# Making P and Q of chunk 5 behind the last stage of chunk 0 instead of behind its first

## The chip, the cores and the metric

The kernel runs on one core of a Trainium2 chip. The metric is device time in microseconds of one launch, the median of the runs shown. In the text PE is TensorE, DVE is VectorE, ACT is ScalarE, POOL is GpSimd, and SP is SyncE, which here does nothing but issue DMAs.

## The reference

Three parts follow one another. The first is a recurrence over 768 time steps with a 40x40 state for each of 32 heads (4 batches of 8), the second and the third are two feed-forward blocks over the 3072 tokens.

```python
for t in range(S):
    y[:, :, t] = np.einsum('bhd,bhde->bhe', rt, state)
    Sa = np.einsum('bhde,bhe->bhd', state, at)
    state_decay = state * wt[:, :, None, :] - np.einsum('bhd,bhe->bhde', Sa, bt)
    state = state_decay + np.einsum('bhd,bhe->bhde', vt, kt)
...
h = (x @ w1) * (x @ w2) @ w3      # moe:  3072x320, 320x1024, 1024x1024
x = h @ w_out                     #       1024x320
out = np.maximum(x @ w_in, 0) ** 2 @ w_out2   # moe2: 320x2048, 2048x320
```

## The kernel before

**The recurrence in chunks.** The 768 steps are cut into 24 chunks of 32 (C = 32). What a chunk needs that does not depend on the state is prepared ahead, mostly six chunks ahead, and what depends on the state is a chain of stages, one chunk after the other.

The preparation of chunk p has three steps. `prep` (L819) loads a tile `im` with k, b and a of the chunk and a tile `iw` with its decays, runs two scans on DVE (`suf`, L556, and `wi`, L566) and multiplies their results into `im` (L578 and L584, on POOL from chunk 4 on). `prep_pq` (L588), called "pq" in the tables, makes P and Q: 32 matmuls over `im` into a PSUM tile `pat` (L597), a copy of P by ACT into `Pn` (L601), a transpose of Q by DVE into `qt` (L602), a mask by POOL (L604) and a store to `Q_d` in DRAM (L605). `prep_kb` (L607), "kb", transposes k and b on PE (L614), copies them on ACT to `kn` (L618) and stores them in `KB_d` (L619). The tiles `im` (except chunks 1, 2, 3 and 5), `iw`, `suf`, `wi`, `qt` and `kn` exist once, so the next chunk waits until the last reader of the one before is done. Four chunks together then go through a triangular solve on DVE (L656, L659).

The chain of chunk c is `do_x0` (PE L742, copy to X0 by ACT L744), `do_sa` (PE L752, ACT L754), `do_sat` (PE L759, ACT L764 and L761, which write `YI` and `vs`), `do_l` (PE L772, DVE L777 writes `YI`), for c > 0 `do_z` (PE L785, ACT L788 writes `YR`), and `do_ys` (PE L800 in two halves). `do_ys` ends on DVE: L808 writes the new state into `RX`, on which the next chunk's `do_x0` waits, and L812 writes the output. For the first four chunks the solve works on halves of 16 steps, and `corner` (PE L690 and L693, ACT L697 and L701) completes the inverse. All PSUM tiles of the chain and of the preparation rotate over two buffers of the name `pat`.

**Filling.** Between the stages PE gets independent work from a queue: the product of w3 and w_out ("fold", L462, into `pw`), then the first feed-forward block (L370, L428), and at the end the weights of the second block. The weights come as 64-bit words and are decoded: a DMA to a tile `raw` or `early` (L319, 512 KB each), two passes on ACT (L325 and L326), two on DVE (L328 and L330), and for w1 and w2 also a cast on ACT (L340) and a difference on POOL (L341). Of `raw` there are three buffers, of the decoded w1 and w2 tiles (`wst`, tag "split") two, and the `early` tiles are two pairs that are used twice.

**What sets the order.** On PE the order is that in which the code is written (manual_schedule). On ACT, DVE, POOL and SP a scheduler decides, from the priorities that the code gives and from a timeline of its own in which it plays the kernel; each engine then takes its instructions strictly in that order. So the place of a PE instruction can move instructions on the other four engines. Which preparation stands between which stages of the first four chunks is in the table BETWEEN (L32): a key is a chunk and the stage behind which the listed steps are called (by `more`, L881, through `run`, L846).

Of the kernel before, what the change touches and what calls it, by code (L numbers as in the profile page):

```python
# [30 lines left out]
)  # L31
BETWEEN = {  # L32
    (0, "start"): (("prep", 5), ("prep", 6)),
    (0, "x0"): (("corner", 0), ("pq", 5)),
    (0, "sat"): (("corner", 1, 0),),
    (0, "l"): (("corner", 1, 1),),
    (0, "ys"): (("kb", 5), ("pq", 6), ("kb", 6)),
    (1, "start"): (("prep", 7),),
    (1, "sat"): (("corner", 2, 0),),
    (1, "l"): (("corner", 2, 1),),  # L40
# [1096 lines left out]
```

## Time and profile before

| | us |
|---|---|
| median of 3 runs | 1073.65 (1069.87 to 1074.45) |
| profiled execution, its own time | 1071.28 |
| its span, first to last instruction | 1069.5 |
| PE busy in the span | 918.1 (86%) |
| DVE busy | 712.5 (67%) |
| ACT busy | 443.8 (41%) |
| POOL busy | 233.2 (22%) |

The mean clock granted to PE is 0.961 of full speed. The chain that ended last goes for 48% of the span over PE, for 26% over DVE and for 12% over DMAs. The kernel has three parts in time: to about 59 us only preparation, to about 690 us the 24 chunks with the filling between them, and from about 740 us the second feed-forward block, in which PE is busy almost all the time. The change lies at the start of the second part.

How to read it: an engine's row gives the start, the duration, the line, and out<-in by the names in the code; in brackets stands how long the engine was idle before it and what ended that. An idle engine costs time only where the chain waits for it.

### The profile page before, as it was taken

The page shows a single profiled execution, that of the slowest core. Times are in us where ns is not written, and L with a number is a line of the kernel's source. Part 1 is how long each engine was busy: PE and PEld are TensorE (multiplying, and loading weights), DVE is VectorE, ACT ScalarE, POOL GpSimd, SP SyncE. Part 2 cuts the span into 40 slices and gives each one's busy share as a digit, 9 for nine tenths or more (in the row PEclk, how much of TensorE's full clock was granted, in tenths as well). Part 3 has the DMA queues.
Part 4 walks back from the last instruction along what each step waited for, and adds up shares of the span by engine and source line. Part 5 has one row for each costly group of instructions (what it writes and reads, how often), then busy time and mean ns, then how long its engine had stood idle before and what let it go on. Part 6 is the DMA issues. An engine that isn't in the chain of part 4 may idle for free.

```text
span 1069.5 us, 29225 instructions
## 1 busy us (share of the span) xinstructions
PE 918.1 (86%) x12240; PEld 822.5 (77%) x12240; DVE 712.5 (67%) x1399; ACT 443.8 (41%) x942; POOL 233.2 (22%) x304
## 2 busy tenths in 40 slices
PE   1327777688989889979899999889999999999997
PEld 1315545588888878979798889868989898898896
DVE  6864879957975997798489444887456554444432
ACT  2424556343434423424343434775334333333332
POOL 0271224433343343533200000652000000000000
PEclk9999888899999999989899999989999999999999
DMA  8976785666666567766644542665122121000001
GB/s 212 307 235 177 209 247 158 171 168 170 163 154 173 148 151 182 170 170 149 164 118 110 136 96 60 171 188 111 30 62 53 59 48 25 2 25 1 18 8 28
DMA packets 208922, 134.45 MB, mean 126 GB/s; under 512 B 143741, under 2 KB 184062, under 8 KB 208368
## 3 DMA queue, kind: packets, MB, share of 16 engines
q1 hardware_dynamic: 201424, 110.61, 40.6%
q0 software_dynamic: 7072, 21.57, 7.1%
q8 instruction: 99, 1.62, 0.7%
q10 hardware_dynamic: 288, 0.33, 0.2%
q14 instruction: 39, 0.32, 0.1%
HBM read 99.27 MB, written 33.19 MB: 124 GB/s over the span
## 4 chain that ended last, share of the span: by engine, by line
PE 48%; DVE 26%; DMA 12%; issue 5%; ACT 4%; POOL 3%; SPq 2%; ACTq 0%; DVEq 0%; POOLq 0%
PE ph L370 16%; PE po L997 15%; PE ab L370 6%; DMA im<-img 5%; DVE tmp L656 4%; PE px L428 4%; DVE T L659 4%; PE pat L800 2%; DVE RX L808 2%; DVE yst L812 2%; DVE gl L408 2%; DVE g L402 1%; DVE wst L328 1%; DVE YI L777 1%; POOL im L584 1%
## 5 line engine op out<-in xcount | busy, mean ns | idle before, releaser
L997 PE MATMUL po<-wul,rh 128*128 128x320 f32 x384 | 118.3, 308 | 0.0
L997 PE MATMUL po<-wuh,rh 128*128 128x320 f32 x384 | 118.0, 308 | 0.0
L997 PE MATMUL po<-wuh,rl 128*128 128x320 f32 x384 | 116.9, 308 | 0.0
L407 ACT CAST gh<-g 128x256 fp32r<-128x256 f32 x96 | 39.0, 406 | 99.8 <-DVE g L402 86.5
L370 PE MATMUL ph<-xh,wih 128*128 128x512 f32 x192 | 76.0, 396 | 0.7 <-issue 0.7
L428 PE MATMUL px<-wph,gh 128*128 128x320 f32 x192 | 68.1, 355 | 9.3 <-DVE x L433 4.8
L370 PE MATMUL ph<-xh,wil 128*128 128x512 f32 x192 | 75.7, 394 | 0.0
L370 PE MATMUL ph<-xl,wih 128*128 128x512 f32 x192 | 75.6, 394 | 0.0
L997 PEld LDWEIGHTS po<-wul,rh 128*128 128x128 f32 x384 | 72.0, 188 | 4.2
L997 PEld LDWEIGHTS po<-wuh,rh 128*128 128x128 f32 x384 | 72.0, 188 | 3.8
L997 PEld LDWEIGHTS po<-wuh,rl 128*128 128x128 f32 x384 | 71.6, 188 | 0.6 <-DVE rl L984 0.6
L800 PE MATMUL pat<-YI,YR 128*40 128x72 f32 (+1 forms) x1536 | 58.8, 240 | 13.7 <-DVE qt L602 8.1
L800 PEld LDWEIGHTS pat<-YI,YR 128*40 128x40 f32 x1536 | 54.5, 127 | 19.2 <-DVE qt L602 9.7
L408 DVE TENSOR_TENSOR gl<-g,gh 128x256 fp32r<-128x256 f32 x96 | 48.2, 503 | 30.0 <-ACT gh L407 29.6
L401 ACT COPY a_sb<-ab 128x256 f32<-128x256 f32 x96 | 35.6, 371 | 76.4 <-PE ab L370 75.9
L656 DVE TENSOR_TENSOR tmp<-PT,T 128x31 f32<-128x31 f32 (+20 forms) x170 | 64.9, 382 | 3.4
L659 DVE TENSOR_TENSOR T<-T,tmp 128x31 f32<-128x31 f32 (+20 forms) x170 | 64.5, 380 | 3.0
L428 PE MATMUL px<-wph,gl 128*128 128x320 f32 x192 | 63.2, 329 | 3.4 <-DVE gl L408 3.4
L584 POOL TENSOR_TENSOR im<-im,suf 104x256 f32<-104x256 f32 x80 | 64.4, 836 | 0.0
L428 PE MATMUL px<-wpl,gh 128*128 128x320 f32 x192 | 62.4, 325 | 0.0
L370 PE MATMUL ph<-xq,wir 128*128 128x512 f32 x192 | 60.1, 394 | 0.0
L370 PE MATMUL ab<-xh,w1h 128*128 128x256 f32 x192 | 57.9, 302 | 2.5 <-ACT xh L357 2.2
(539 smaller groups left out, 2444.3 us busy)
## 6 DMA issues: line engine op xcount, KB each, us to landing
raw<-w3t SPq DMA_DIRECT2D x16, 512.0 KB
YR<-KB_d SPq DMA_DIRECT2D x48, 160.0 KB
im<-img POOLq DMA_DIRECT2D x28, 240.0 KB, 4.5
wt<-AW_d SPq DMA_DIRECT2D x24, 214.5 KB
raw<-wo SPq DMA_DIRECT2D x16, 320.0 KB
RX<-vp SPq DMA_DIRECT2D x24, 208.0 KB
vs<-rv SPq DMA_DIRECT2D x24, 208.0 KB
KB_d<-kn POOLq DMA_DIRECT2D x14, 320.0 KB, 5.3
```

Source lines behind the costliest of these rows:

```text
L370: mm(out=ps, lhsT=seq[i][0], rhs=seq[i][1], start=(i == 0), stop=(i == 7))
L401: act.copy(out=a_sb, in_=ps[:, 0])
L407: act.copy(out=t["gh"][:, ff], in_=g)
L408: dve.tensor_tensor(out=t["gl"][:, ff], in0=g, in1=t["gh"][:, ff], op=ALU.subtract)
L428: mm(out=ps, lhsT=a_, rhs=b_, start=(k == 0 and i == 0), stop=(k == 7 and i == 2))
L584: eng.tensor_tensor(out=kb[:, g, :, :, j], in0=kb[:, g, :, :, j], in1=sg, op=ALU.mult)
L656: dve.tensor_tensor(out=tv, in0=Pv[:, :, s, s + 1:n].unsqueeze(3).to_broadcast(sh), in1=Tv[:, :, s, 0:s + 1].unsqueeze(2).to_broadcast(sh) ...
L659: return dve.tensor_tensor(out=o, in0=o, in1=tv, op=ALU.subtract).ins
L800: mm(out=ps[64 * y:64 * y + D, b, 72 * z:72 * z + n], lhsT=YR[:, u], rhs=YI[:, u, 0:n], start=True, stop=True, tile_position=(0, 64 * y))
L808: dve.tensor_tensor(out=o, in0=v[r, :, :, C:72], in1=decay.unsqueeze(3).to_broadcast([D, 2, HZ, D]), op=ALU.mult)
L812: dve.tensor_tensor(out=yst[r, :, 2 * g:2 * g + 2].rearrange("p z b t -> p b z t"), in0=v[r, :, :, 0:C], in1=wt[c][r, 2 * g:2 * g + 2, :, ...
L997: mm(out=po[j][g], lhsT=a_, rhs=b_, start=(ff == 0 and i == 0), stop=(ff == 15 and i == 2))
```

## The change

In the table BETWEEN the step ("pq", 5) is moved from behind the stage x0 of chunk 0 to behind its stage ys, where it stands ahead of ("kb", 5). Nothing else is written.

```diff
 BETWEEN = {
     (0, "start"): (("prep", 5), ("prep", 6)),
-    (0, "x0"): (("corner", 0), ("pq", 5)),
+    (0, "x0"): (("corner", 0),),
     (0, "sat"): (("corner", 1, 0),),
     (0, "l"): (("corner", 1, 1),),
-    (0, "ys"): (("kb", 5), ("pq", 6), ("kb", 6)),
+    (0, "ys"): (("pq", 5), ("kb", 5), ("pq", 6), ("kb", 6)),
```

On PE, in chunk 0, the difference (- before, + now) reads:

```order
 L693 MATMUL pat<-x_683,early 16x16 x32
-L597 MATMUL pat<-im 32x64 x32
 L752 MATMUL pat<-X_101,tt 32x40 x32
 L759 MATMUL pat<-idt,SA 104x128 x4
 L690 MATMUL pat<-tt,early 32x16 x32
 L772 MATMUL pat<-RT,vs 64x64 x16
-L693 MATMUL pat<-x_837,early 16x16 x32
+L693 MATMUL pat<-x_799,early 16x16 x32
 L800 MATMUL pat<-YI,YR 40x72 x32
 L462 MATMUL pw<-wo_sb,wst 128x320 x2
+L597 MATMUL pat<-im 32x64 x32
 L614 MATMUL pat<-idt,im 128x104 x8
```

The 32 matmuls of P and Q of chunk 5 stood ahead of `do_sa` of chunk 0 and now stand behind its `do_ys`.

The scheduler follows with other orders on the other engines, from chunk 0 to chunk 5 and once more, slightly, at the start of the second block. On SP, behind the last stage of chunk 0, there stood in before (qt_1032 is Q of chunk 6, kn_987 belongs to chunk 5, im_105 is the load of chunk 7, early_1741 holds pieces of w1 and w2):

```order
L723 DMA wt_984<-AW_d_90 104x528
L815 DMA X_d_60<-yst_932 40x4x128
L619 DMA KB_d_92<-kn_987 128x640
L319 DMA early_1741<-w1 128x1024
L541 DMA im_105<-img 40x1536 x2
L605 DMA Q_d_91<-qt_1032 128x256
```

and now (qt_981 is Q of chunk 5):

```order
L723 DMA wt_946<-AW_d_90 104x528
L815 DMA X_d_60<-yst_894 40x4x128 x2
L319 DMA early_1741<-w1 128x1024
L319 DMA early_1741<-w2 128x1024
L619 DMA KB_d_92<-kn_987 128x640
L605 DMA Q_d_91<-qt_981 128x256
L541 DMA im_105<-img 40x1536 x2
```

A second early load of 512 KB and the store of Q of chunk 5 have come ahead of the load of chunk 7.

On ACT, in chunk 1, there stood between X0 and `vs` in before (early_1741 had been loaded behind chunk 0):

```order
L744 ACTIVATE X0_101<-pat_1067 128x320
L325 ACTIVATE wst_590<-raw_591 128x512
L325 ACTIVATE wst_1742<-early_1741 128x512
L326 ACTIVATE early_1741<-early_1741 128x512
L754 COPY SA_102<-pat_1108 128x8x40
L764 COPY YI_506<-SA_102 32x8x40 x4
L761 COPY vs_891<-pat_1152 104x4x4x32
```

and now:

```order
L744 ACTIVATE X0_101<-pat_1067 128x320
L326 ACTIVATE early_1775<-early_1775 128x512
L340 CAST w1h_1735<-wst_1759 128x512
L325 ACTIVATE wst_590<-raw_591 128x512
L754 COPY SA_102<-pat_1108 128x8x40
L764 COPY YI_506<-SA_102 32x8x40 x4
L325 ACTIVATE wst_1767<-early_1758 128x512
L326 ACTIVATE early_1775<-early_1775 128x512
L326 ACTIVATE raw_1292<-raw_1292 128x512
L761 COPY vs_853<-pat_1152 104x4x4x32
```

The decoding passes over the tiles early_1775 and raw_1292, which in before came later in the row than `vs`, now stand ahead of it. On SP the loads of the two are issued now behind the store of Q of chunk 6 and behind the multiplied `im` of chunk 7.

## Rows read from the trace of the kernel before

**Rows 1.** Busy time by stretch: start:end, length, engines with counts, PE clock, DMA share, GB/s.

```profile
100.00:120.00 20.00, 12.36 (x265) 9.28 (x266) 13.64 (x19) 13.43 (x29) 5.44 (x6) 0.88 0.82 235
180.00:200.00 20.00, 16.26 (x268) 12.18 (x268) 19.62 (x34) 11.48 (x25) 8.58 (x9) 1.00 0.41 112
740.00:1069.00 329.00, 322.50 (x1789) 290.39 (x1787) 153.71 (x221) 119.51 (x198) 0.00 (x0) 1.00 0.13 29
```

**Rows 2.** PE in order of time, chunk 0: start, duration, row, idle before and its releaser.

```profile
72.59 1.18 PE L597 MATMUL pat<-im 40*32 40x64 f32 x64 [9.93 <-POOL im L578]
73.70 1.29 PE L752 MATMUL pat<-X,tt 32*32 32x40 f32 x64
...
89.27 4.07 PE L800 MATMUL pat<-YI,YR 128*40 128x72 f32 x64 [0.89 <-PE pat L693]
```

**Rows 3.** ACT in order of time, the corner of chunk 0.

```profile
62.72 1.07 ACT L701 COPY tt<-pat 16x128 f32<-16x128 f32 x4 [0.83 <-PE pat L693]
```

**Rows 4.** DVE in order of time, chunk 0.

```profile
80.12 1.26 DVE L566 TENSOR_TENSOR_SCAN wi<-iw,inv 104x528 f32<-104x528 f32 x1 [2.80 <-DMA AW_d<-wi]
...
83.99 1.26 DVE L556 TENSOR_TENSOR_SCAN suf<-iw,mark 104x529 f32<-104x529 f32 x1 [2.27 <-DMA iw<-img]
...
85.85 1.26 DVE L566 TENSOR_TENSOR_SCAN wi<-iw,inv 104x528 f32<-104x528 f32 x1
87.78 1.39 DVE L777 TENSOR_TENSOR YI<-pat,msk 64x512 f32<-64x512 f32 x2 [0.67 <-PE pat L772]
91.45 0.99 DVE L808 TENSOR_TENSOR RX<-pat,gc 40x320 f32<-40x320 f32 x2 [2.29 <-PE pat L800]
```

**Rows 5.** SP's issues in order of time: start and time of the issue.

```profile
97.99 0.49 SPq L319 DMA_DIRECT2D early<-w  x1
98.58 0.71 SPq L541 DMA_DIRECT2D im<-img  x2
99.60 0.35 SPq L605 DMA_DIRECT2D Q_d<-qt  x1
...
106.52 0.35 SPq L319 DMA_DIRECT2D early<-w  x1
```

**Rows 6.** The chain that ended last, in order of time: start, length, what.

```profile
98.95 7.54 DMA im<-img
...
130.71 7.13 DMA im<-img
...
141.54 8.36 DMA raw<-w3t
```

**Rows 7.** ACT in order of time, chunks 1 and 2.

```profile
102.18 0.46 ACT L744 ACTIVATE X<-pat 128x320 f32<-128x320 f32 x1
...
106.70 0.59 ACT L761 COPY vs<-pat 104x512 f32<-104x512 f32 x1
107.31 0.62 ACT L340 CAST w1h<-wst 128x512 fp32r<-128x512 f32 x1
...
111.57 0.67 ACT L325 ACTIVATE wst<-early 128x512 f32<-128x512 f32 x1 [2.72 <-DMA early<-w]
...
117.68 1.40 ACT L788 COPY YR<-pat 40x640 f32<-40x640 f32 x2 [2.11 <-PE pat L785]
...
142.31 0.41 ACT L359 CAST xq<-xr 128x256 fp32r<-128x256 f32 x1 [2.32 <-DMA xr<-X_d]
```

**Rows 8.** POOL in order of time, the product into im of chunk 7.

```profile
107.79 3.08 POOL L584 TENSOR_TENSOR im<-im,suf 104x256 f32<-104x256 f32 x4
```

**Rows 9.** DVE in order of time, chunk 1.

```profile
110.91 2.30 DVE L556 TENSOR_TENSOR_SCAN suf<-iw,mark 104x529 f32<-104x529 f32 x1 [0.57 <-POOL im L584]
113.13 0.66 DVE L330 SCALAR_TENSOR_TENSOR wst<-raw,wst 128x512 uint32<-128x512 uint32 x1
...
114.52 1.39 DVE L777 TENSOR_TENSOR YI<-pat,msk 64x512 f32<-64x512 f32 x2
```

**Rows 10.** PE in order of time, the last stage of chunks 1 and 2.

```profile
121.07 2.66 PE L800 MATMUL pat<-YI,YR 128*40 128x72 f32 x64
...
167.04 3.53 PE L800 MATMUL pat<-YI,YR 128*40 128x72 f32 x64 [3.29 <-ACT kn L618]
```

## The prediction

> **What bounds the kernel now.** I read the busy time by stretch first. From 740 us on PE is busy for 322.5 of 329 us [rows 1], a fixed amount of work in a fixed order; whatever moves its start moves the end by as much. The change sits at 60 to 90 us, so the question is whether a gain there comes through to 740 us. Second I read PE in chunk 0. The matmuls of P and Q of chunk 5 wait 9.93 us for POOL's product into their `im`, and `do_sa` of chunk 0, which needs nothing from them, starts behind them at 73.70 [rows 2]; its own inputs are ready when ACT ends the corner, at 62.72 + 1.07 = 63.8 [rows 3]. That is the wait which goes: 9.9 us. Third I read DVE and SP there, for what is late next, and last ACT in chunk 1, since its order changes most.
>
> **What is removed, and what is late next.** `do_sa` can start about 9.9 us earlier. In the chain of chunk 0 the next fixed point is DVE's first scan at 80.12, which waits for a store of the scan before it and ends at 81.38 [rows 4]. `L777` stands behind it in the new order, as its `do_l` on PE is done by then: it starts at 81.4 instead of 87.78, a lead of 6.4. The next fixed point is the second pair of scans; the first of them waits for a DMA that is issued when the scan at 80.12 has read its tile, and it starts at 83.99 in either order. The pair ends at 85.85 + 1.26 = 87.1 [rows 4], and `L808` of chunk 0 now stands behind it: 87.1 instead of 91.45. **The lead at the end of chunk 0 is 4.3 us.** Of the 9.9, 5.6 go into waits on DVE that the moved matmuls had covered.
>
> **What is added behind chunk 0.** The same 32 matmuls now run there, 1.18 us where they run cold [rows 2]; they cost the chain about as much, since k and b of chunk 5 and P and Q of chunk 6 queue behind them for the two PSUM buffers. The load of chunk 7 waits for the last of these and for SP: ahead of it now come one more early load (0.49 us to issue) and the store of Q of chunk 5 (0.35) [rows 5]. So it leaves 4.3 - 0.8 = 3.5 us earlier, the second half at 98.95 - 3.5 = 95.45. It took 7.54 us in before [rows 6], with one early load just ahead of it [rows 5]. With the same landing it is there at 103.0. If it must wait for the extra 512 + 128 KB at the 235 GB/s of that stretch [rows 1], which is 2.7 us, it is there at 105.7. Before it was 106.5. I take the middle, 104.3.
>
> The trace shows the load landing 7.54 us behind its issue with 512 KB issued just ahead of it [rows 5, 6]. The Trainium skill, page "DMA: Bandwidth & Descriptors", section "Queues, rings and completion order", says that each DMA engine takes the descriptors of one queue in ring order, and all these loads are SP's. By that rule the upper value, 105.7, would hold and everything in chunk 1 would come 1.4 us later than I sum it; no row of before decides between the two.
>
> **What moves on ACT, chunk 1.** Here I expect the lead to be lost. In before nothing that waits for a DMA stands between X0 and `vs`: X0 at 102.18, `vs` at 106.70 [rows 7]. Now the passes over early_1775 and raw_1292 stand ahead of `vs`. The load of raw_1292 needs a buffer that is freed by a decode on DVE behind the scan `suf` of chunk 8, and that scan needs POOL to be done with chunk 7. Step by step: landing 104.3; POOL done (107.79 + 3.08) - 106.49 = 4.4 us later [rows 6, 8], 108.7; the scan 2.30 and the decode 0.66 [rows 9], 111.7; the load, taken as long as the early one from 106.52 to 111.57, 5.05 [rows 5, 7], 116.7; the pass on ACT, 0.67 like L325 [rows 7]. **`vs` of chunk 1 comes at 117.4 instead of 106.70.** The early_1775 pass ends sooner than this.
>
> Before, `L777` of chunk 1 waited for the scan and started at 114.52 [rows 9], so much of the 10.7 us was slack. Now it follows `vs` by 0.59, two casts of 0.62, one decode pass on ACT of 0.67 [rows 7] and two on DVE of 0.66 [rows 9], 3.8 us: 121.2, that is 6.7 later. The last decode frees the buffer for the next raw load, whose pass stands ahead of the copy to `YR`: 121.2 + 5.05 + 0.67 + 1.40 = 128.3 [rows 5, 7]. `YR` began at 117.68 and `do_ys` at 121.07 in before [rows 7, 10], with 2 us of filling between, which is done by then now. **`do_ys` of chunk 1 starts at 128.3, 7.2 us later than before.** Its ends: with the earlier landing of chunk 7 and both raw loads as short as the 2.6 us from the end of the scan at 81.38 to 83.99 [rows 4], a much smaller load, 7.2 - 1.3 - 4.9 = +1; with the later landing, +8.6.
>
> **What chunk 2 gives back.** The loads that now delay chunk 1 are loads for which chunk 2 waited: it had two early loads more and a raw load of 8.36 us on the chain [rows 6]. In the new order that raw load follows the store of `im` of chunk 8 with no other weight load just ahead; at 5.05 us it gives 3.3 back. The pass for which `xq` waited 2.32 us [rows 7] now stands behind the copy of SA, which waits for a load issued later instead; I count that at nothing. `do_ys` of chunk 2 was at 167.04 [rows 10] and comes 7.2 - 3.3 = 3.9 later. From there DVE is busy for 19.62 of 20 us [rows 1] with decodes and the solve, the same work in both, so a delay is neither made up nor enlarged. At the start of the second block the scheduler's differences let the last transpose pass one decode step; I count them at nothing, since they change what DVE does first and not how much.
>
> **The sum.** The profiled execution took 1071.28 us (span 1069.5 and 1.8 around it); 1071.28 + 3.9 = 1075.2. It lies 2.4 below the median of the runs, 1073.65, so for the median I expect 1073.65 + 3.9 = 1077.5.
>
> **The rivals.** *The lead stays (faster).* The weight loads come in one stream through three buffers, and DMA is already busy for 0.82 of 100 to 120 us [rows 1]. If that stream and not ACT's order sets the end of chunk 2, the loads issued earlier in the new order make it no later, chunk 2 returns all of the 7.2, and the 4.3 of chunk 0 remain: 1069.3; if DVE's own lead of 6.4 at `L777` also remains, 1067.2. Against it: raw loads need decoded buffers, and the decode stands behind the scan of chunk 8 in chunk 1. It decides if `vs` of chunk 1 comes before about 110. *Nothing remains (same).* The stream ends where it did, chunk 0's lead becomes idle time: 1073.65. *The waits grow (slower).* In the new order a raw load stands ahead of the load of chunk 8 too, which took 7.13 us on the chain [rows 6]; with the upper value of chunk 1 and nothing given back it is +8.6: 1082.3. It decides if `do_ys` of chunk 2 is more than 6 us late, that is behind 173.
>
> **How the numbers follow.** The forecast, 3.9 later, has a chance of 0.35, with a range of its own of 1074 to 1080. The lead stays: 0.20. Nothing remains: 0.17. The waits grow: 0.28. A measurement of this kernel can tell about 0.5% from no change, 5.4 us. Faster by more needs the lead to stay almost whole, three quarters of its chance: 0.15. Slower by more is the growing waits and the upper end of the forecast: 0.28 + 0.05 = 0.33. The rest, 0.52, is within. The range for 8 in 10 reaches from the lead that stays, with a little to spare, to above the growing waits: 1068 to 1084.
>
> **What would show it.** In the changed profile `do_sa` of chunk 0 should start near 64, `L777` near 81.4 and `L808` near 87.1, with the scans at 80.12 and 85.85 unmoved. In chunk 1 the ACT rows ahead of `vs` should show idle time that ends with DMAs early and raw, `vs` should be near 117 and `do_ys` near 128, in chunk 2 near 171, and the second block should start some 4 us later. The prediction is wrong if ACT passes those rows without waiting, or if a delay at 171 is gone at 740.

## The result, and the profile after

The changed kernel takes 1082.46 us, the median of seven runs. Six lie between 1077.66 and 1084.84; one of 1734 us was disturbed and is left out of the ratio. The kernel before took 1074.2 us beside it. The ratio is 1.0076, 95% interval 1.0052 to 1.0100: slower, by about 8 us. In a second set of runs, on the chip of the last experiments, it was 1.0101 (1.0057 to 1.0146). The predicted time was 1077.5 us and the range 1068 to 1084 holds the result; "slower by over 0.5%" had been given 0.33, less than "within 0.5%" with 0.52. The profiled execution is the slowest of the six, 1084.84 us with a span of 1083.0, so its later stages show some 2 us more than the median; its chunk 0 also starts 1.1 us later than that of before (`do_x0` at 60.13 instead of 59.03).

Busy time by stretch, to be read against [rows 1]: start:end, length, PE, PEld, DVE, ACT and POOL with counts, PE clock, DMA share, GB/s.

```profile
100.00:120.00 20.00, 9.62 (x212) 6.48 (x212) 10.96 (x15) 10.27 (x20) 8.20 (x8) 0.76 0.63 202
...
740.00:1083.00 343.00, 334.88 (x1858) 301.47 (x1856) 162.49 (x235) 124.86 (x208) 2.37 (x3) 0.99 0.14 33
```

From 740 us on PE is as full as before. In the 20 us from 100 on, chunk 1, every engine but POOL does less than before: PE 9.62 us instead of 12.36, DVE 10.96 instead of 13.64, ACT 10.27 instead of 13.43, the DMA engines 0.63 instead of 0.82. They wait for each other.

PE in order of time, to be read against [rows 2, 10]: start, duration, row, idle before and its releaser.

```profile
63.90 1.84 PE L752 MATMUL pat<-X,tt 32*32 32x40 f32 x48 [0.37 <-ACT tt L701]
...
104.72 1.30 PE L742 MATMUL pat<-RX,XL 128*32 128x40 f32 x64 [9.33 <-ACT kn L618]
...
131.88 2.90 PE L800 MATMUL pat<-YI,YR 128*40 128x72 f32 x64
...
175.89 4.07 PE L800 MATMUL pat<-YI,YR 128*40 128x72 f32 x64 [4.21 <-DVE qt L602]
```

DVE, against [rows 4]:

```profile
80.93 1.26 DVE L566 TENSOR_TENSOR_SCAN wi<-iw,inv 104x528 f32<-104x528 f32 x1 [2.92 <-DMA AW_d<-wi]
82.22 1.39 DVE L777 TENSOR_TENSOR YI<-pat,msk 64x512 f32<-64x512 f32 x2
...
87.92 0.99 DVE L808 TENSOR_TENSOR RX<-pat,gc 40x320 f32<-40x320 f32 x2
...
91.70 0.45 DVE L602 STREAM_TRANSPOSE qt<-pat 128x256 f32<-128x256 f32 x1
102.09 0.69 DVE L328 SCALAR_TENSOR_TENSOR wst<-wst,early 128x512 uint32<-128x512 uint32 x1 [9.93 <-ACT early L326]
...
104.06 0.69 DVE L328 SCALAR_TENSOR_TENSOR wst<-wst,early 128x512 uint32<-128x512 uint32 x1 [0.56 <-ACT early L326]
104.67 0.44 DVE L602 STREAM_TRANSPOSE qt<-pat 128x256 f32<-128x256 f32 x1
```

Chunk 0 is done earlier, as meant. Then PE stands idle for 9.33 us ahead of `do_x0` of chunk 1 (L742), which starts at 104.72; before it started at 97.84. It needs one of the two `pat` buffers, and the preparation of chunk 6 holds both: one has k and b until ACT has copied them into `kn` (103.93 + 0.74 = 104.67), the other has P and Q until DVE has transposed Q into `qt` (104.67 + 0.44 = 105.11). `do_x0` starts 0.05 us behind the end of the copy and before the transpose is done, so here it waits for the buffer of `kn`, as its row says. In the kernel before it took the other one: it started at 97.84, and `kn` of chunk 6 was copied only at 101.54.

ACT, against [rows 7], and SP's issues, against [rows 5]:

```profile
100.85 0.66 ACT L325 ACTIVATE wst<-early 128x512 f32<-128x512 f32 x1 [5.92 <-DMA early<-w]
...
102.81 0.67 ACT L325 ACTIVATE wst<-early 128x512 f32<-128x512 f32 x1 [0.76 <-DMA early<-w]
103.93 0.74 ACT L618 COPY kn<-pat 128x320 f32<-128x320 f32 x2
...
108.11 0.42 ACT L744 ACTIVATE X<-pat 128x320 f32<-128x320 f32 x1
...
120.25 0.65 ACT L326 ACTIVATE raw<-raw 128x512 uint32<-128x512 uint32 x1 [3.23 <-DMA raw<-w3t]
120.81 0.57 ACT L761 COPY vs<-pat 104x512 f32<-104x512 f32 x1
```

```profile
94.70 0.85 SPq L319 DMA_DIRECT2D early<-w  x2
95.64 0.37 SPq L619 DMA_DIRECT2D KB_d<-kn  x1
96.11 0.38 SPq L605 DMA_DIRECT2D Q_d<-qt  x1
96.58 1.99 SPq L541 DMA_DIRECT2D im<-img  x2
```

SP now issues two loads of 512 KB (parts of w1 and w2) and only then the stores of `kn` and `qt` of chunk 5. Before, the store of `kn` went out ahead of the one such load there, and the store of `qt` of chunk 5 had gone out at 83.34. The passes over these two loads stand on ACT ahead of `kn` of chunk 6, and the two L328 behind them stand on DVE ahead of the transpose. The chain that ended last (start, length, what) now runs through one of these loads, its pass and `kn` to `do_x0`:

```profile
95.12 7.67 DMA early<-w
```

### The profile page after: what moved, and what is told of

The parts are those of the page before. It is cut to its first block, busy times and chain, and to the rows that moved or that the text cites. A ratio compares the mean times of both kernels' runs of the same rounds, so it can differ in the third digit from the quotient of the medians.

```text
span 1083.0 us, 29230 instructions
## 1 busy us (share of the span) xinstructions
PE 921.7 (85%) x12240; PEld 823.2 (76%) x12240; DVE 713.8 (66%) x1399; ACT 441.7 (41%) x942; POOL 234.9 (22%) x304
## 4 chain that ended last, share of the span: by engine, by line
PE 45%; DVE 27%; DMA 16%; ACT 4%; issue 4%; SPq 2%; POOL 1%; ACTq 0%; DVEq 0%; POOLq 0%
PE ph L370 16%; PE po L997 15%; PE ab L370 5%; DVE tmp L656 4%; DVE T L659 4%; DMA im<-img 3%; PE px L428 2%; DVE RX L808 2%; DVE yst L812 2%; DMA early<-w 2%; PE pat L800 2%; DVE gl L408 2%; DMA AW_d<-wi 2%; DMA raw<-win 2%; DVE wst L328 1%
## 5 line engine op out<-in xcount | busy, mean ns | idle before, releaser
L800 PE MATMUL pat<-YI,YR 128*40 128x72 f32 (+1 forms) x1536 | 57.0, 236 | 17.8 <-DVE qt L602 14.5
L800 PEld LDWEIGHTS pat<-YI,YR 128*40 128x40 f32 x1536 | 52.5, 124 | 23.1 <-DVE qt L602 16.7
L659 DVE TENSOR_TENSOR T<-T,tmp 128x31 f32<-128x31 f32 (+20 forms) x170 | 66.9, 393 | 3.1
L408 DVE TENSOR_TENSOR gl<-g,gh 128x256 fp32r<-128x256 f32 x96 | 45.9, 478 | 29.7 <-ACT gh L407 29.2
```

The costliest lines, as they stand in the source:

```text
L408: dve.tensor_tensor(out=t["gl"][:, ff], in0=g, in1=t["gh"][:, ff], op=ALU.subtract)
L659: return dve.tensor_tensor(out=o, in0=o, in1=tv, op=ALU.subtract).ins
L800: mm(out=ps[64 * y:64 * y + D, b, 72 * z:72 * z + n], lhsT=YR[:, u], rhs=YI[:, u, 0:n], start=True, stop=True, tile_position=(0, 64 * y))
```

## The experiments

Three theories were held against each other. **A**, the prediction's: the passes over w1 and w2 that the planner now puts ahead of the chain's copies on ACT. **B**: the products this late in the chunk are dear by themselves. **C**: the bytes loaded ahead of the load of chunk 7. After the first four runs came **D**: there is one `qt`; with chunks 5 and 6 back to back the second transpose waits until the first one's store has landed, and that store queues behind the two loads. As first stated, D has `do_x0` wait for the buffer of that transpose. The traces add that `kn` is single too, that its store queues behind the same loads, and that it differs from run to run for which of the two buffers `do_x0` waits: in the changed kernel, e3, e8 and e11 it starts 0.05 us behind the copy `kn` of chunk 6, in the kernel before and in all other runs before that copy has begun. The table has for each run the ratio to the kernel before with its 95% interval, the median, and the start in its profiled execution of `do_x0`, X0 and L800 (the stage `do_ys`) of chunk 1 and of L800 of chunk 2. From chunk 5 on single profiles drift by some us (e9 stood at +2.0 us in chunk 7, at -0.5 in chunk 12 and at +5.7 in chunk 23), so chunks 1 and 2 are read from the profiles and the rest from the ratios.

| run | ratio | median us | `do_x0` 1 | X0 1 | L800 1 | L800 2 |
|---|---|---|---|---|---|---|
| before | 1 | 1071.7 to 1074.4 | 97.84 | 102.18 | 121.07 | 167.04 |
| changed | 1.0076 (1.0052 to 1.0100) | 1082.46 | 104.72 | 108.11 | 131.88 | 175.89 |
| e1 | 0.9973 (0.9949 to 0.9996) | 1069.70 | 95.66 | 100.44 | 119.19 | 163.96 |
| e2 | 1.0074 (1.0047 to 1.0101) | 1079.01 | 97.22 | 104.58 | 125.04 | 168.77 |
| e3 | 1.0143 (1.0112 to 1.0173) | 1086.46 | 103.03 | 104.39 | 124.47 | 170.11 |
| e4 | 1.0051 (1.0023 to 1.0078) | 1077.42 | 98.08 | 102.62 | 118.70 | 167.71 |
| e5 | 1.0047 (1.0017 to 1.0076) | 1075.13 | 96.28 | 103.81 | 125.13 | 163.17 |
| e6 | 1.0001 (0.9972 to 1.0029) | 1072.60 | 97.93 | 102.31 | 121.17 | 167.33 |
| e7 | 1.0063 (1.0030 to 1.0095) | 1079.01 | 97.61 | 105.87 | 124.09 | 171.91 |
| e8 | 1.0109 (1.0070 to 1.0148) | 1083.32 | 105.44 | 108.82 | 131.41 | 176.52 |
| e9 | 1.0008 (0.9981 to 1.0035) | 1075.19 | 98.88 | 100.24 | 127.12 | 168.70 |
| e10 | 0.9987 (0.9959 to 1.0015) | 1072.92 | 97.00 | 101.12 | 127.02 | 171.04 |
| e11 | 1.0101 (1.0057 to 1.0146) | 1084.27 | 104.30 | 107.75 | 129.93 | 174.21 |
| e12 | 1.0051 (1.0020 to 1.0081) | 1077.38 | 94.34 | 99.04 | 116.81 | 166.00 |

**e1: the products just ahead of the last stage**

```diff
-    (0, "l"): (("corner", 1, 1),),
-    (0, "ys"): (("pq", 5), ("kb", 5), ("pq", 6), ("kb", 6)),
+    (0, "l"): (("corner", 1, 1), ("pq", 5)),
+    (0, "ys"): (("kb", 5), ("pq", 6), ("kb", 6)),
```

> The P and Q products of chunk 5 (L597, 32 matmuls) stand just ahead of the last stage of chunk 0 (L800) instead of just behind it; all else on TensorE is as in the changed kernel. The planner now leaves ScalarE, SyncE and GpSimd of chunk 1 in the order of the kernel before: no pass over the staged w1 and w2 (L325, L326 on early) ahead of the copy X0 of chunk 1. Theory A (the loss comes from these passes, which wait for their loads ahead of the chain's copies): do_sa of chunk 0 near 64 us as in the changed kernel, L800 of chunk 0 between 84 and 87, do_x0 of chunk 1 between 94 and 97 (97.84 in the kernel before, 104.72 in the changed one), L800 of chunk 1 between 116 and 121, the time 1067 to 1072 us, ratio 0.993 to 0.999. Theory B (products this late in chunk 0, with the one qt buffer and the two pat buffers, cost it by themselves): do_x0 of chunk 1 behind 100, L800 of chunk 1 behind 126, the time 1078 to 1085 us.

One step earlier on PE, and the loss is gone: 1069.7 us, under both kernels. `do_sa` of chunk 0 starts at 64.22, so the wait for POOL is gone here too. PE, DVE, ACT and SP of this run:

```profile
84.08 1.17 PE L597 MATMUL pat<-im 40*32 40x64 f32 x64 [1.92 <-DVE YI L777]
...
95.66 0.84 PE L742 MATMUL pat<-RX,XL 128*32 128x40 f32 x64
```

```profile
88.32 0.45 DVE L602 STREAM_TRANSPOSE qt<-pat 128x256 f32<-128x256 f32 x1
...
95.15 0.45 DVE L602 STREAM_TRANSPOSE qt<-pat 128x256 f32<-128x256 f32 x1 [2.27 <-ACT Pn L601]
```

```profile
99.80 0.75 ACT L618 COPY kn<-pat 128x320 f32<-128x320 f32 x2 [4.74 <-DMA KB_d<-kn]
100.44 0.46 ACT L744 ACTIVATE X<-pat 128x320 f32<-128x320 f32 x1
```

```profile
95.16 0.36 SPq L619 DMA_DIRECT2D KB_d<-kn  x1
...
96.10 0.71 SPq L319 DMA_DIRECT2D early<-w  x1
```

The two transposes are 7 us apart and the second waits for no store; `do_x0` goes at once; `kn` of chunk 6 waits for the store of `kn` of chunk 5, which is issued ahead of the load and lands in 4.6 us. B is out: products that come 11.5 us later than in the kernel before (72.59 there [rows 2]) cost nothing here; that the place of the changed kernel, behind L800, costs nothing by itself either is seen in e9. A and D are not yet told apart, since the planner put ACT back into its old order as well.

**e2: one step earlier still**

```diff
-    (0, "l"): (("corner", 1, 1),),
+    (0, "l"): (("pq", 5), ("corner", 1, 1)),
```

and `("pq", 5)` out of `(0, "ys")` as in e1.

> The P and Q products of chunk 5 stand one step earlier still, ahead of the second half of chunk 1's corner (L693). By this the planner again puts two passes over the staged w1 and w2 ahead of the copy X0 of chunk 1 on ScalarE, as in the changed kernel. Theory A: do_x0 of chunk 1 may go early, but its copy X0 waits for the passes: X0 of chunk 1 behind 104 us, L800 of chunk 1 behind 126, the time 1078 to 1086 us although the products are made earlier than in the run beside it. Theory B (the later the products, the more it costs): faster than the run with the products just ahead of L800, at most 1075 us.

The products are earlier than in e1 and the kernel is 1% slower than e1, so B's rule, the later the products the more it costs, does not hold. `do_x0` goes at 97.22, but X0 comes at 104.58 behind two passes that wait for their loads, and L800 of chunk 1 at 125.04, 1 us before what A said. That is A, but chunk 0 has no lead here either: L800 of chunk 0 starts at 88.63 (89.27 before), having waited 4.15 us for the first transpose.

**e3 and e4: the passes held, in the changed kernel and in the kernel before**

```diff
+                with tc.issue_after(late[-1]) if tag == "split" and late else nullcontext():
-                act.activation(out=o, in_=hi.bitcast(F32), func=AF.Copy, scale=2.0 ** -112)
-                act.activation(out=lo, in_=lo, func=AF.Copy, scale=2.0 ** -29, bias=LOW)
+                    act.activation(out=o, in_=hi.bitcast(F32), func=AF.Copy, scale=2.0 ** -112)
+                    act.activation(out=lo, in_=lo, func=AF.Copy, scale=2.0 ** -29, bias=LOW)
```

with `late` holding the copy `YR` of chunk 1.

> The changed kernel; on ScalarE the passes over the staged w1 and w2 (L325, L326 on early) are held behind the copies YR of chunk 1. TensorE's order and the two loads of w1 and w2 ahead of the load of chunk 7 stay as in the changed kernel. Theory A: do_x0 of chunk 1 back from 104.72 to between 94 and 98 us, X0 of chunk 1 before 100, vs of chunk 1 before 114, L800 of chunk 1 before 125, the time at most 1076 us unless the passes held back cost as much later. Theory C (the two loads of 1 MB in all ahead of the load of chunk 7 delay the chain by their bytes): do_x0 early, but suf of chunk 8 still behind 113 and L800 of chunk 1 behind 129, the time over 1079 us.

> Control: the kernel before with the same passes held behind the copies YR of chunk 1. There they stand behind X0 of chunk 1 already. Theory A: L800 of chunk 1 between 117 and 122 us (121.07 in the kernel before), the time within 0.5% of the kernel before, 1068 to 1078 us. If holding the passes is a gain or a loss by itself, whatever P and Q do, it shows here as well and has to be taken off the run of the changed kernel with passes held.

A falls as the only cause of the late `do_x0`: without any pass ahead of it, it comes at 103.03 instead of 104.72, and the time does not fall at all. Holding the passes costs 0.5% by itself (e4), and taking that off leaves e3 0.9% slower, the loss of the change. C, as it was written, is out as well, though its time came in: the scan `suf` of chunk 8 went at 108.26, far ahead of 113, and L800 of chunk 1 at 124.47, ahead of 129. What stands there now, on PE, DVE, ACT and SP of e3 (its lines are one or two further down: L744 is `do_x0`, L604 the transpose, L620 `kn`, L320 the loads):

```profile
103.03 1.29 PE L744 MATMUL pat<-RX,XL 128*32 128x40 f32 x64 [8.44 <-ACT kn L620]
```

```profile
90.44 0.45 DVE L604 STREAM_TRANSPOSE qt<-pat 128x256 f32<-128x256 f32 x1
102.59 0.45 DVE L604 STREAM_TRANSPOSE qt<-pat 128x256 f32<-128x256 f32 x1 [11.70 <-DMA Q_d<-qt]
```

```profile
102.23 0.75 ACT L620 COPY kn<-pat 128x320 f32<-128x320 f32 x2 [8.46 <-DMA KB_d<-kn]
```

```profile
93.36 0.85 SPq L320 DMA_DIRECT2D early<-w  x2
94.31 0.37 SPq L621 DMA_DIRECT2D KB_d<-kn  x1
94.78 0.38 SPq L607 DMA_DIRECT2D Q_d<-qt  x1
```

The transpose of chunk 6 waits 11.70 us for the store of the one of chunk 5, whose issue at 94.78 lies 7.8 us before. The copy `kn` waits 8.46 us for the store of `kn` of chunk 5, issued 7.9 us before, and `do_x0` follows the end of that copy (102.23 + 0.75 = 102.98). The transpose ends at 103.04, so the other buffer would have come free no sooner. The passes had covered these two waits: in the changed kernel they are named, here the stores are.

**e5 and e6: a second buffer for `qt`, in the changed kernel and in the kernel before**

```diff
-                qt = first(c, "qt", [128, 2, HZ, C], {1: (at, "yst"), 3: (at, "yst")})
+                qt = first(c, "qt", [128, 2, HZ, C], {1: (at, "yst"), 3: (at, "yst"), 5: (ma, "xf")})
```

> The changed kernel with a second buffer for qt: the transposed product of chunk 5 goes into the space of xf, which is not yet in use, so the one of chunk 6 needn't wait until the store Q_d of chunk 5 has landed. Theory D (the wait for qt: with chunk 5 and 6 now back to back, the transpose of chunk 6 waits for the store of chunk 5, and do_x0 of chunk 1 waits for the pat buffer that this transpose holds): do_x0 of chunk 1 between 94 and 97 us instead of 104.72, and the transpose of chunk 6 (L602) before 97 instead of 104.67. The planner still leaves two passes over the staged w1 and w2 ahead of kn of chunk 6 and of X0 on ScalarE, as in the run with the products ahead of the corner, so by theory D X0 of chunk 1 lies near 104.6, L800 of chunk 1 near 125 and the time between 1075 and 1081 us. Theory A (these passes alone set do_x0): do_x0 of chunk 1 stays behind 101 and the time within 3 us of the changed kernel.

> Control: the kernel before with the second buffer for qt. There the two transposes lie 16 us apart and no row shows a wait for it, so by every theory nothing changes: do_x0 of chunk 1 within 1 us of 97.84, the time within 0.3% of the kernel before.

PE, DVE and ACT of e5:

```profile
96.28 1.27 PE L742 MATMUL pat<-RX,XL 128*32 128x40 f32 x64
```

```profile
91.93 0.45 DVE L602 STREAM_TRANSPOSE qt<-pat 128x256 f32<-128x256 f32 x1
95.22 0.45 DVE L602 STREAM_TRANSPOSE qt<-pat 128x256 f32<-128x256 f32 x1 [2.84 <-ACT Pn L601]
```

```profile
100.56 0.66 ACT L325 ACTIVATE wst<-early 128x512 f32<-128x512 f32 x1 [5.38 <-DMA early<-w]
...
103.19 0.72 ACT L618 COPY kn<-pat 128x320 f32<-128x320 f32 x2
103.81 0.44 ACT L744 ACTIVATE X<-pat 128x320 f32<-128x320 f32 x1
```

`do_x0` goes at 96.28, 8.4 us earlier, 7 us ahead of the copy `kn` that the changed kernel's row had named: it now has the buffer of the transpose, which is done at 95.67. So this edit takes away the wait for `qt` and also changes which buffer `do_x0` waits for; it does not show that `kn` had no part in the wait of the changed kernel. The kernel before is not moved by the same buffer (1.0001). The ratio falls from 1.0076 and 1.0101 to 1.0047. What is left stands on ACT: X0 at 103.81, behind the two passes and `kn`.

**e7: both, and e8: the store on another queue.** e7 has the edits of e3 and e5 together; e8 only this one:

```diff
-                q_["prep"].dma_start(out=Q_d[c], in_=qf.rearrange("p h t -> p (h t)"))
+                (pool if c == 5 else q_["prep"]).dma_start(out=Q_d[c], in_=qf.rearrange("p h t -> p (h t)"))
```

> The changed kernel with the second buffer for qt and, as in the earlier pair of runs, the passes over the staged w1 and w2 held behind YR of chunk 1. Theory D: do_x0 of chunk 1 between 93 and 97 (103.03 with the passes held alone), L800 of chunk 1 between 115 and 120 (124.47 with the passes held alone, 118.70 in the kernel before with them held), the time at most 1080 us, within 4 us of the kernel before with the passes held (1077.42) and at least 5 us under the changed kernel with them held (1086.46). If the wait for qt is not the cause, L800 of chunk 1 stays behind 123 and the time over 1083 us.

> The changed kernel with the store of qt of chunk 5 to Q_d issued by GpSimd, right behind its mask, and not by SyncE behind the two loads of w1 and w2. The orders of ScalarE and VectorE stay those of the changed kernel, in which the transpose of chunk 6 stands behind two passes (L328) that wait for those loads. If the landing of the store alone sets do_x0 of chunk 1, it goes to between 94 and 98 us and the time falls under 1078 us. If the order on VectorE sets it as well (two causes side by side, so that taking away either one gives little), the transpose of chunk 6 stays between 101 and 105, do_x0 of chunk 1 gains at most 3 us, and the time stays between 1079 and 1086 us.

e7 meets D in the time (1079.01, with the kernel before at 1077.42 under the same hold), misses its range for `do_x0` by 0.6 us (97.61), and misses it in L800 of chunk 1: 124.09 instead of 115 to 120, behind the 123 that was to speak against D. ACT shows why:

```profile
105.23 0.75 ACT L620 COPY kn<-pat 128x320 f32<-128x320 f32 x2 [8.72 <-DMA KB_d<-kn]
```

The store of the one `kn` stands behind the same two loads; X0, at 105.87, queues behind `kn` on ACT. In the profiled pair e3 and e7 this takes back the gain of `do_x0` whole (L800 of chunk 1 at 124.47 and 124.09); the medians differ by 7 us all the same, and that difference is not shown by these two profiles.

In e8 the store leaves early, and nothing is gained; the transpose is 0.4 us later than the range given for it (PE and DVE):

```profile
105.44 1.30 PE L742 MATMUL pat<-RX,XL 128*32 128x40 f32 x64 [10.09 <-ACT kn L618]
```

```profile
104.78 0.69 DVE L328 SCALAR_TENSOR_TENSOR wst<-wst,early 128x512 uint32<-128x512 uint32 x1 [0.72 <-ACT early L326]
105.40 0.44 DVE L602 STREAM_TRANSPOSE qt<-pat 128x256 f32<-128x256 f32 x1
```

So the transpose is held twice over: by the store (e3) and by the passes in front of it (e8), and taking away one leaves it at 102.6 or 105.4. `do_x0` itself waits for `kn` in e8, which the edit does not touch, so this run does not tell what the store of `qt` alone is worth to it. `kn` is held twice over as well: by the passes (103.93 in the changed kernel) and by the store of `kn` of chunk 5 (102.23 in e3). All these holds come from the same two loads.

**e9 and e10: the loads behind the stores, with one and with two `qt`**

```diff
+                with tc.issue_after(late[-1]) if tag == "split" and late else nullcontext():
-                for p, f, src in parts:
-                    sp.dma_start(out=rv_[p, f], in_=src)
+                    for p, f, src in parts:
+                        sp.dma_start(out=rv_[p, f], in_=src)
```

with `late` holding the store `KB_d` of chunk 6; e10 has the edit of e5 as well, and the same orders on ACT and SP.

> The changed kernel with the loads of w1 and w2 (L319) held on SyncE behind the store KB_d of chunk 6, so that the stores Q_d and KB_d of chunk 5 go out ahead of them. Theory D with its place (the stores that free qt and kn queue behind two loads of 512 KB, and the passes over these loads hold ScalarE and VectorE as well): the transpose of chunk 6 (L602) goes from 104.67 to between 98 and 101 us, as it still waits for the store of chunk 5 but that lands some 4 us after its issue; do_x0 of chunk 1 between 98 and 101, X0 of chunk 1 between 99 and 103 (108.11 in the changed kernel), the time between 1071 and 1078 us. If the loads ahead are not what delays, do_x0 of chunk 1 stays behind 103 and the time over 1079 us.

> The run beside it with the second buffer for qt; the orders of ScalarE and SyncE are the same in both, so the pair shows the wait for qt alone. Theory D: the transpose of chunk 6 before 97 and do_x0 of chunk 1 between 94 and 97; X0 of chunk 1 stands behind kn of chunk 6, which waits for the store KB_d of chunk 5, so it stays between 98.5 and 102 and gains at most 2 us on the run beside it; the time between 1069 and 1077 us, 0 to 3 us under the run beside it. If qt does not matter, do_x0 of chunk 1 is equal in both within 1 us.

PE, SP, DVE and ACT of e9, its lines two or three further down (L745 `do_x0`, L604 the transpose, L620 `kn`, L747 X0):

```profile
98.88 1.29 PE L745 MATMUL pat<-RX,XL 128*32 128x40 f32 x64 [3.03 <-DVE qt L604]
```

```profile
94.98 0.36 SPq L607 DMA_DIRECT2D Q_d<-qt  x1
95.44 0.37 SPq L621 DMA_DIRECT2D KB_d<-kn  x1
```

```profile
98.38 0.45 DVE L604 STREAM_TRANSPOSE qt<-pat 128x256 f32<-128x256 f32 x1 [5.00 <-DMA Q_d<-qt]
```

```profile
99.13 0.75 ACT L620 COPY kn<-pat 128x320 f32<-128x320 f32 x2 [3.73 <-DMA KB_d<-kn]
100.24 0.44 ACT L747 ACTIVATE X<-pat 128x320 f32<-128x320 f32 x1 [0.35 <-PE pat L745]
...
107.24 0.66 ACT L327 ACTIVATE wst<-early 128x512 f32<-128x512 f32 x1 [3.94 <-DMA early<-w]
```

This is the run that decides. PE's order is that of the changed kernel, `qt` and `kn` are single, and with the two stores ahead of the loads they land 3.4 and 3.7 us behind their issue, `do_x0` goes at 98.88, X0 at 100.24, and the kernel is as fast as before (1.0008), while the changed kernel beside it on the chip (e11) stands at 1.0101. With the loads the passes over them come later too; what the stores and what the passes are worth by themselves this run does not tell apart. The second `qt` then adds 1.9 us at `do_x0`, as expected, and nothing at X0; e9 and e10 don't differ in time by more than their intervals. In e9 a pass still waits 3.94 us for its load on ACT, now ahead of SA and `vs`, and L800 of chunk 1 is 6.1 us late; 4.4 of these come back in chunk 2.

**e11 and e12: the changed kernel again, and e1 with the loads held**

> The changed kernel itself, on the chip of the runs beside it, since its comparison with the kernel before (1.0076) is from another set of runs than that with the second qt buffer (1.0047). All theories: ratio 1.005 to 1.010, time 1078 to 1086 us, do_x0 of chunk 1 between 102 and 106.

> P and Q of chunk 5 just ahead of the last stage of chunk 0 (the first of these runs, 1069.7 us) and the loads of w1 and w2 held behind the store KB_d of chunk 6. There the stores of chunk 5 are ahead of these loads already, so by theory D little is left to gain: X0 of chunk 1 between 98 and 100.5 (100.44), L800 of chunk 1 between 116 and 119.5, the time 1066 to 1072 us. If loads and their passes, later now, hold up chunks 1 to 4, the time goes over 1073 us.

e11 repeats the loss. e12 is the control for e9: where the stores of chunk 5 are ahead of the loads already, holding the loads back makes X0 of chunk 1 1.4 us earlier and the kernel 7.7 us slower than e1 (1077.38 against 1069.70). X0 and L800 of chunk 1 lie in the ranges given, the time lies over the 1066 to 1072 that D had, and over the 1073 that was to mean that the later loads hold up the chunks behind. So later loads are no gain by themselves; the 9 us by which e9 is faster than e11 come from what the loads stood in front of. Where e12 loses its time after chunk 1 (4.3 us ahead of the kernel before at L800 of chunk 1, 1.0 at that of chunk 2) was not followed up. A kernel with a second buffer for `kn` as well, without either wait but with the loads where the planner puts them, was not run.

## Why the prediction was right and where it failed

**The wait removed, and the lead of chunk 0: right.** `do_sa` at 63.90 (said: 63.8), L777 at 82.22 (81.4), L808 at 87.92 (87.1), with the scan at 80.93 the next fixed point as said; the last two are 0.8 us late, and this chunk 0 starts 1.1 us late. Of the 9.8 us that `do_sa` gained, 3.5 are left at L808 (said: 4.3).

**What is added behind chunk 0: the step that failed.** I costed the 32 matmuls at their own 1.18 us (they took 0.85 there; the granted clock is 1.00 around both, so it does not show what "cold" meant) and wrote that the later products "queue behind them for the two PSUM buffers". I followed the store of Q of chunk 5 only as 0.35 us of SP's time ahead of the load of chunk 7. I did not ask who waits for the stores of chunk 5 to land, which now go out behind two loads, and who waits for the passes over these loads. It is the one `kn` and the one `qt`, and through them the two `pat` buffers, of which `do_x0` needs one; in the changed kernel it waited for that of `kn`. That term is 6.9 us at `do_x0` of chunk 1 and stands nowhere in the sum. Before, the two transposes lie 16 us apart, so that no row shows such a wait for `qt` (DVE, kernel before). For `kn` a row does show it, 4.29 us with X0 behind it on ACT, and I passed it over:

```profile
81.29 0.42 DVE L602 STREAM_TRANSPOSE qt<-pat 128x256 f32<-128x256 f32 x1
...
97.34 0.45 DVE L602 STREAM_TRANSPOSE qt<-pat 128x256 f32<-128x256 f32 x1 [2.10 <-issue]
```

```profile
101.54 0.76 ACT L618 COPY kn<-pat 128x320 f32<-128x320 f32 x2 [4.29 <-DMA KB_d<-kn]
```

That the two transposes had come together stood in the two orders alone.

**The load of chunk 7: no longer the bound.** I ran the chain of chunk 1 through its landing. Its second half, from which I reckoned, was issued at 98.06, 0.9 us earlier (said: 3.5), but POOL began on that chunk at 107.46, behind the mask of `qt` and the low part of w1, without waiting for it.

The rule that I weighed for this load shows at another one. The store of `qt` landed 7.8 us behind its issue with the two loads ahead of it (e3) and 3.4 us without (e9). The Trainium skill, page "DMA: Bandwidth & Descriptors", section "Queues, rings and completion order", has each DMA engine take the descriptors of one queue in ring order; by that rule a small store pays for the loads issued before it, and these rows agree.

**ACT of chunk 1: right in place, wrong in weight.** The rows ahead of `vs` wait for early and raw loads as said, and `vs` comes at 120.81 (said: 117.4), L800 at 131.88, +10.8 (said: 128.3, +7.2). But the raw load took 3.5 us and not the 5.05 of my sum (issued at 116.72, pass at 120.25); the delay came in ahead of it, with X0 at 108.11 instead of 102.18. And e9 shows that passes ahead of SA and `vs` alone, with L800 of chunk 1 6.1 us late, cost the kernel nothing that can be measured.

**What chunk 2 gives back: mis-sized.** 2.0 us (10.8 to 8.9) instead of 3.3; e9 gave back 4.4. After chunk 2 the delay was to stay as it was; the profiled execution has +11.0 in chunk 4 and +11.5 in chunk 23, e11 +9.0 and +7.6. I can't tell a rule from that.

**The rival that came in.** L800 of chunk 2 at 175.89 is behind the 173 from which "the waits grow" was to decide, and its 1082.3 us is the measured time. Its mechanism, a raw load ahead of the load of chunk 8, is not new in the changed kernel: before, one went out just ahead of that load as well (129.70, 130.22), and POOL began on chunk 8 7.8 us behind the issue of its load, now 8.5 us (140.00, 148.49). So the time fits by the rival's size, not by its reason. The forecast's own range, 1074 to 1080, does not hold the measured time; that the wide range does, and that slower was the right way, is luck as far as the reason goes. "The lead stays" is what e1 has: 3.1 us at L800 of chunk 2, 1069.7 us.

## What to carry to other kernels

When a step is moved next to its own next instance, look at every single buffer that the step and its neighbours write (here the staging tiles of two stores) and at the queue through which these buffers are emptied: the price of this move came from the landing of those stores and from the loads ahead of them, not from the matmuls. Where a planner orders the rest, place the moved step at two or three neighbouring points and compare the orders of the queues, for here one place earlier on PE was worth about 1% (a ratio of 0.9973 against 1.0076 and 1.0101). A small store that frees a buffer on the chain should leave ahead of large loads in the same queue.

## What the runs showed that I had not expected

A wait can hide behind another with the same root: the changed kernel's rows named passes and the copy `kn` for the late `do_x0`, removing the passes left that copy waiting for a store and changed 1.7 us, moving the other store alone gained nothing, and moving the common root, two loads, gave the time back. Which of two rotating buffers a stage waits for can change with an edit elsewhere: that `do_x0` ran ahead of `kn` in e5 said nothing against the row of the changed kernel, where it waited for it. And the same edit, loads held back by one store, was worth -0.9% in the changed kernel and +0.8% in e1.
